# A gated sum of chunked attention and a long convolution on one core: another written order of the same steps

## The chip, the core and the metric

The kernel runs on one core of a Trainium2 chip. The core has TensorE (matmuls, "PE" in the profile; "PEld" is its weight load), Vector ("DVE"), Scalar ("ACT"), GpSimd ("POOL") and SyncE ("SP", which issues all DMAs here). The metric is device time in microseconds of one execution. Three runs of the kernel before gave 381.07, 383.3 and 385.4 us; the median is 383.3.

## What is computed

The reference takes x (2048 tokens, 512 columns, bf16) and mixes two results by a gate per token:

```python
g = sigmoid((x * gate_w).sum(-1, keepdims=True))
return g * A(x) + (1 - g) * B(x)
```

A is attention over four segments of 512 tokens with 32 heads of 16 columns. Within a segment it is causal softmax attention; what earlier segments left is read from a running state M (16x16 per head, from phi(k) and v, phi(t) = t+1 for t > 0, else exp(t)) and mixed in per head by sigmoid(beta). Then `@ wo`.

B is a state-space convolution: per column d a kernel K[d, l] = Re sum_n C P^l dB with 128 complex states n, and y = causal convolution of x with K over 2048 tokens (an FFT of length 4096 in the reference), plus x * Dskip.

## The kernel before

**Attention.** Each segment s and group hg of 8 heads has the steps: projections `pk`, `pq` (four 128x512 matmuls each), five score blocks `sc` that fill PSUM banks 0 to 3 together, one Scalar exponential of 128x2048 per block (L1021), products with v (`pv`, 17 columns per head so that the sum of weights falls out), `nrm` on Vector (L993 to L996: reciprocal, product, product), the state step `st`/`sm`, the state's read `mem` (L1071 to L1075) and a transpose `oT`. Per segment there are also `xT` (transposes of x), `tok` (v) and `gate`.

**The convolution's kernel.** `prep` computes exp(dt*A) by exponential and sine; `pow0`, `pow1` square it again and again for the two halves of the columns (L751 to L753), `pwc` converts each power (L759 to L763). For each quarter c of the columns, `tab`c builds two tables F and G of powers, by 13 complex products, each of three Vector instructions:

- L1118: table = table entries x one part of the power
- L1121: t2 = the same entries x the other part
- L1125: table = table + t2

The third reads both earlier ones; the second doesn't read the first. `lag`c then multiplies F and G by 256 small matmuls of 128x20 and evicts the result. F and G exist once, so `tab`(c+1) may begin to overwrite them only when `lag`c's matmuls are done.

**The convolution.** `xl1` makes the first level of a transform of x and stores it in a scratch tensor scr_Z in DRAM. The tail reads it back in 16 steps t: `Zx` loads 256 KB, `X` are two matmuls, their result is copied with its two 64-partition halves swapped by two DMAs (sb<-sb), `CT` loads 448 KB of constants (c_DN), `K` transforms the convolution's kernel, `Y` (L1220) is the product, `V` transforms back and is stored in V2 by a DMA. Zx and CT have three buffers each. `fin` adds attention's result `@ wo` and the skip term into a PSUM bank, `fir` adds the last level over all of V2, an eviction multiplies by the gate, and the result is stored. The tail's buffers M2 and V2 lie over F and G, those of CT and Zx over the powers, so the `X` steps follow `lag3`.

**What sets the order.** `build_graph` records 1679 steps, each with its dependencies and the tiles it touches. The string ORDER lists them by number; a letter behind the number (a or v) puts a free eviction on Scalar (L240) or Vector (L241). `Sched.replay` walks the string: each engine's program is the listed order of its own steps, and SP's queue the listed order of the DMAs. A tile takes a slot of its pool when its first step is walked and gives it back after its last. `Pool.take` chooses the slot that became free longest ago, `Psum.take` the bank (or pair) free longest ago out of 4 to 7, and banks 0 to 3 only before the first score block and after the last. `Sched.emit` then puts a semaphore wait before a step for each producer that isn't known to be done, also for a producer on the same engine, other than TensorE.

```python
o.alld = list(o.deps)
for T in o.wt:
    o.alld += list(T.prev)
...
if d.eng == o.eng and o.eng == "PE":
    continue
if know.get(d.sem, 0) >= d.val:
    continue
o.waits.append(d)
```

Of the kernel before, what the change touches and what calls it, by code (L numbers as in the profile page):

```python
# [24 lines left out]
class Pool:  # L25


    def __init__(self, name, addr, size, n=1, phase=1):
        self.name, self.addr, self.size, self.n, self.phase = name, addr, size, n, phase
        self.free = [(0, i, ()) for i in range(n)]  # L30
        self.left = 0
        self.last = {}
        self.blockers = ()
        self.idx = -1

    def take(self, tile, now):
# [10 lines left out]
    def give(self, tile, now):  # L47
        self.free.append((now, tile.slot, tuple(tile.users)))
        self.last[tile.slot] = tile.users
        self.left -= 1  # L50


class Psum:


    def __init__(self):
        self.free = {b: (0, ()) for b in range(8)}
        self.wide = self.begun = self.ended = 0

    def take(self, tile, now):  # L60
        best = None
        low = self.begun == 0 or self.ended == self.wide or len(tile.banks) == 1
        for cand in tile.banks:
            if all(b in self.free and (low or b > 3) for b in cand):
                t = max(self.free[b][0] for b in cand)
                if best is None or t < best[0]:
                    best = (t, cand)
        cand = best[1]
        tile.prev = [o for b in cand for o in self.free[b][1]]
        for b in cand:  # L70
            del self.free[b]
        tile.slot, tile.cand = cand[0], cand
        self.begun += len(tile.banks) == 1

    def give(self, tile, now):
        self.ended += len(tile.banks) == 1
        for b in tile.cand:
            self.free[b] = (now, tuple(tile.users))
# [34 lines left out]
class Sched:  # L113
# [37 lines left out]
    def ps(self, width=1, dt=F32, banks=None):  # L151
# [5 lines left out]
        self.psum.wide += len(banks) == 1  # L157
# [91 lines left out]
    def replay(self, order):  # L249
# [4 lines left out]
        for now, (i, e) in enumerate(order):  # L254
            o = self.ops[i]
            if o.alts:
# [12 lines left out]
            for T in o.tiles:  # L269
                T.nuse -= 1  # L270
                if T.nuse == 0:
                    T.pool.give(T, now + 1)
# [100 lines left out]
192 53 0 204 8 394 9 14 12 13 54 10 56 11 55a 15 22 28 57v 16 3 26 23a 1 24 17 27v 25a 1234 29 30 202 376 32 31 33 4  # L373
34 252 203a 18 35 36 44 2 199 253a 37 39 20 38 40 249 19 41 200a 42 21 43 201 211 172 5 173 7 218 219 45 6 47 207 48
46 49 52 58 209 174 50 175 61a 51 220 67v 68 69 66 176 59 60 72 212v 70 239 62 64 63 240 71 188 82 84 65 205 85a 83 78
241 86 87 189 190 191 193 76 227 194 97a 228 77 210a 98 99 94 208v 195 229 73v 213 74 75 95 96 106 108 235 90 206a 236
107 109v 118 221 120 237 119 133v 134 135 110 111 121a 196 79v 222 130 80 122 223 123 88 131 132 91a 234 144 224 238
89 102 242 177 243 178 142 225 100 179 226 230 143 145a 157v 154 156 103a 158 155 159 197 101 250a 114 112 1240 146
115a 147 113 124 126 104 127a 105 125 136 138 116 214 117 137 139a 150 180 148 166a 149 160 162 181 163a 161 92 169a
93 198 128 1002a 170 1003a 171 1008 1004a 129 251 1005a 215 261 1006a 1007 1241a 1010 262 1011 151a 1012 182 1009 1242  # L380
263 1016 183 184 1235 185 186 187 1017 1018 1236a 1022 265 1243a 1023 266 1244 1024 1237 267 1013 295 1014 1015 216
164 165 1238a 81 140 270 141 296a 271 231 1239 232 233 217 272 1025 292 377 1026 293a 278 378a 279 1027 379 280 1255
264 268 1038 269 273 274 380a 282 275 276 283 294 244 245 254 246 284 1245 152 153 1019 247 1020 1021 1028 248a 306
1029 255 307 1246a 1030 256 1247 257 308 277 1034 281 258 1037 1248a 311 1249 259 312 260 1039 1250 313 1252 1035 336
1276 1036 1251a 302 1253a 303 333 337a 167 1254 168 304 1031 1266 1268 1032 285 286 287 288 334a 289 319 1033 1267a
320 290 321 305 1040 309 291v 310 314 1256 1041 1258 1042 1269a 323 1043 1257a 324 1044 1270 1259a 1045 297 318 335
325 322 315 1260 316 1046 317 1047 1048 1049 298 345 1050v 346 299 1051 347 300 1052 1053 1054 301 1060v 1061v 1062v
1063a 1064v 349 1055a 1068 350 1069 1056 1070 1261 1074 351 1263 1057 326 1075 327 1058 1076 1078 1059 328 329 330
1262a 354 1080 1264a 355 1081 331 1265 356 386 1082 348 1083 352 353 332a 362 1084 387a 363 389 364 1271 1085 357 390a
358 366 359 1272a 367 360 393 391 1273 388 1092 338 591 368 1277 392 1093 1274a 408 339 1094 1275 409 1278a 1279 410  # L390
397 340 341 1280v 1065 1281 1066 1067 412 398a 1071 413 1072 342 1073 414 399 1077 343 344 443 1079 1086 400a 361 1087
425 444a 426 365 1088 427 401 1089 395 1090 402a 1091 429 396a 430 445 1098 411 431 1099 446 1100 1101 1282 1102 369
370 1103 447a 415 609 371 417 1283a 372 450 418 373 448 1095 374 419 1284 381 416 449 382 375v 493 1096 1285a 462 383
384 1286 463 494a 385 424 495 420 464 1097 403 1292 428 432 421 433 422 434 404 435 458 436 1293a 459 423 1104 405 460
1105 406 1106 1107 1109 1108v 1110 475 476 1111 477 1112 461 1113v 407 1118v 1114 1124 1294 1119v 1120v 1121a 1287
1115 1122v 479 1295a 1126 480 1127 1116 1288a 1128 1289 1117 1132 481 465 1133 496 1296 1134 1297 1138 466 1139 1290a
467 497a 468 1291 1140 592 498 500 1141 594 469 806 499 1142 593a 523 524 1143 470 525 1298 1123 1125 1129 1299a 1130
515 1131 595a 516 471 472 473 1300 1135 517 1136 541 1137 1144 1145 1301a 451 1146 542a 1302 1303 452 1147 1305 1304a
1148 1306a 474 506 1149 1307 507 543 1308 453 508 478 454 1310 1156 455 1157 482 1158 483 456 1309a 527 484 1311a 485
528 486 457 1312 437 529 1150 544 1313 438 439 545a 440 510 1314a 511 548 1151 546 441 512 487 1315 547 442v 488 509  # L400
489 1316a 490 565 566 1317 1152 513 567 514 491 522 1153 526 501 530 492a 531 1154 556 502 557 601 558 532 533 534 518
1155 549 602a 560 1159 550 561 1160 604 1161 562 503 504 1162 603 551 1163 552 1164 519 520 605a 1165 521 573 1166a
# [944 lines left out]
```

## Time and profile before

| | before |
|---|---|
| runs | 381.07, 383.3, 385.4 us |
| profiled execution: time, span | 381.07 us, 381.1 us |
| granted TensorE clock, mean | 0.870 |
| Vector instructions, Scalar instructions | 627, 322 (3 of them table loads) |
| matmuls | 4268 |
| DMA: bytes, mean rate | 36.07 MB, 95 GB/s |
| longest releaser of Scalar's evictions (L240) | TensorE, 42.7 us in 47 waits |
| longest releaser of Scalar's exponentials (L1021) | TensorE, 26.4 us in 33 waits |
| median from issue to landing: c_DN, scr_Z read, sb<-sb | 5.5, 5.1, 5.1 us |

"Busy" is time in which an engine executes an instruction; the remainder is idle time, which the profile puts down to whatever semaphore came last. The profile's evictions and matmuls go through helpers, so one line (L646, L240, L241) stands for many steps; steps are told apart by shape and time.

### The profile page before, as it was taken

The page shows a single profiled execution, that of the slowest core. Times are in us where ns is not written, and L with a number is a line of the kernel's source. Part 1 is how long each engine was busy: PE and PEld are TensorE (multiplying, and loading weights), DVE is VectorE, ACT ScalarE, POOL GpSimd, SP SyncE. Part 2 cuts the span into 40 slices and gives each one's busy share as a digit, 9 for nine tenths or more (in the row PEclk, how much of TensorE's full clock was granted, in tenths as well). Part 3 has the DMA queues.
Part 4 walks back from the last instruction along what each step waited for, and adds up shares of the span by engine and source line. Part 5 has one row for each costly group of instructions (what it writes and reads, how often), then busy time and mean ns, then how long its engine had stood idle before and what let it go on. Part 6 is the DMA issues. An engine that isn't in the chain of part 4 may idle for free.

```text
span 381.1 us, 9878 instructions
## 1 busy us (share of the span) xinstructions
PE 298.8 (78%) x4268; PEld 170.4 (45%) x4268; DVE 275.0 (72%) x627; ACT 275.1 (72%) x322; POOL 3.2 (1%) x9
## 2 busy tenths in 40 slices
PE   3856167877696768879955899999969888788994
PEld 3314024455353534556532657655323433334551
DVE  0699999996998499978996352989768687644011
ACT  4599999788995589797965485789947786544242
POOL 1000000000000000000000000000000000000000
PEclk9965559689997586999968696999989999999998
DMA  7900002121200061101005500002797587663113
GB/s 180 321 15 1 3 28 84 64 104 49 84 29 29 3 184 58 57 3 21 2 2 156 204 3 2 2 2 56 233 248 210 172 245 210 187 174 110 34 75 146
DMA packets 25755, 36.07 MB, mean 95 GB/s; under 512 B 9200, under 2 KB 13808, under 8 KB 25584
## 3 DMA queue, kind: packets, MB, share of 16 engines
q1 hardware_dynamic: 25712, 35.45, 31.0%
q8 instruction: 33, 0.54, 0.6%
q14 instruction: 10, 0.08, 0.1%
HBM read 20.10 MB, written 6.29 MB: 69 GB/s over the span
## 4 chain that ended last, share of the span: by engine, by line
DVE 40%; PE 34%; DMA 14%; ACT 5%; issue 5%; SPq 2%; ACTq 0%
PE psum L646 33%; DVE sb L1118 8%; DVE sb L1125 8%; DVE sb L1121 7%; DMA sb<-c_DN 5%; DMA sb<-sb 5%; DMA sb<-scr_Z 3%; DVE sb L241 3%; ACT sb L1021 2%; DVE sb L996 2%; SPq L236 2%; DVE sb L753 1%; DMA sb<-in_B_C_im_dram 1%; DVE sb L752 1%; DVE sb L763 1%
## 5 line engine op out<-in xcount | busy, mean ns | idle before, releaser
L646 PE MATMUL psum<-sb 128*128 128x17 bf16 (+12 forms) x4132 | 287.2, 239 | 68.9 <-ACT sb L1021 21.6
L646 PEld LDWEIGHTS psum<-sb 128*128 128x128 bf16 (+3 forms) x4132 | 159.9, 100 | 193.9 <-issue 46.8
L1021 ACT ACTIVATE sb<-psum 128x2048 bf16<-128x2048 f32 x80 | 150.3, 1879 | 26.9 <-PE psum L646 26.4
L240 ACT ACTIVATE sb<-psum 128x512 bf16<-128x512 f32 (+2 forms) x143 | 85.0, 623 | 49.5 <-PE psum L646 41.4
L241 DVE CAST sb<-psum 128x512 bf16<-128x512 f32 (+1 forms) x66 | 43.7, 675 | 34.1 <-PE psum L646 29.4
L1118 DVE TENSOR_TENSOR sb<-sb 128x512 bf16<-128x512 bf16 (+3 forms) x52 | 35.8, 690 | 0.8
L1125 DVE TENSOR_TENSOR sb<-sb 128x512 bf16<-128x512 bf16 (+3 forms) x52 | 34.7, 669 | 1.5
L1121 DVE TENSOR_TENSOR sb<-sb 128x512 bf16<-128x512 bf16 (+3 forms) x52 | 35.5, 685 | 0.1
L1220 DVE TENSOR_TENSOR sb<-sb 128x1024 bf16<-128x1024 bf16 x32 | 21.7, 687 | 7.7 <-ACT sb L240 4.7
L244 DVE TENSOR_SCALAR sb<-psum,sb 128x512 bf16<-128x512 f32 x5 | 3.8, 751 | 21.4 <-PE psum L646 21.4
L243 ACT ACTIVATE sb<-psum,sb 128x512 bf16<-128x512 f32 x11 | 7.6, 687 | 14.8 <-PE psum L646 14.8
L996 DVE TENSOR_TENSOR sb<-psum,sb 128x256 bf16<-128x256 f32 x32 | 13.4, 423 | 0.9
L1033 DVE TENSOR_TENSOR sb<-sb 128x1024 bf16<-128x1024 bf16 (+1 forms) x20 | 11.5, 573 | 0.0
L751 ACT ACTIVATE sb<-sb 128x512 f32<-128x512 f32 x18 | 11.0, 626 | 0.1
L684 PE MATMUL psum<-sb 128*128 128x128 bf16 x64 | 5.8, 254 | 6.1 <-DMA sb<-c_ident 4.7
L993 DVE RECIPROCAL sb<-psum 128x16 f32<-128x16 f32 x32 | 8.0, 250 | 1.2 <-PE psum L646 1.1
L943 DVE TENSOR_SCALAR sb<-sb 128x512 bf16<-128x512 bf16 x16 | 5.6, 349 | 4.4 <-ACT sb L240 4.4
L759 ACT ACTIVATE sb<-sb 128x512 bf16<-128x512 f32 x14 | 8.7, 620 | 0.0
L952 ACT ACTIVATE sb<-sb 128x512 bf16<-128x512 bf16 x12 | 7.6, 634 | 1.3 <-PE psum L646 1.0
L1075 DVE TENSOR_TENSOR sb<-psum,sb 128x512 bf16<-128x512 f32 x12 | 8.3, 689 | 0.3
L1071 DVE SCALAR_TENSOR_TENSOR sb<-psum,sb 128x32 f32<-128x32 f32 x12 | 2.2, 184 | 8.3 <-PE psum L646 8.3
L684 PEld LDWEIGHTS psum<-sb 128*128 128x128 bf16 x64 | 4.8, 115 | 7.1 <-DMA sb<-c_ident 4.7
(65 smaller groups left out, 116.3 us busy)
## 6 DMA issues: line engine op xcount, KB each, us to landing
sb<-c_DN SPq DMA_DIRECT2D x16, 448.0 KB, 5.5
sb<-in_A_x_dram SPq DMA_DIRECT2D x8, 512.0 KB, 3.7
scr_Z<-sb SPq DMA_DIRECT2D x16, 256.0 KB, 2.0
sb<-scr_Z SPq DMA_DIRECT2D x16, 256.0 KB, 5.1
sb<-sb SPq DMA_DIRECT2D x32, 128.0 KB, 5.1
sb<-sb SPq DMA_DIRECT2D x16, 256.0 KB
out_dram<-sb SPq DMA_DIRECT2D x8, 256.0 KB, 2.1
sb<-c_M SPq DMA_DIRECT2D x1, 1024.0 KB, 6.4
```

The source lines that it names most:

```text
L240: fa = lambda e: e.activation(dst(), src(), ACT.Copy)
L241: fd = lambda e: e.tensor_copy(dst(), src())
L646: mm = lambda e, o_, l, r_, st, sp, **kw: e.matmul(o_, lhsT=l, rhs=r_, start=st, stop=sp, skip_group_check=True, **kw)
L684: i = e.transpose(ap(P, t2 * 512 + k * 128, n=128), ap(xks, (2 * hb + t2) * 512 + k * 128, n=128), ap(ident, n=128))
L751: op("ACT", ("As", 512), lambda e, sq=sq, Z=Z: e.activation(ap(sq, n=512), ap(Z, n=512), ACT.Square), r=[Z], w=[sq], key=PW[h] + PWS * k)
L996: op("DVE", ("V1", 256), lambda e: e.tensor_tensor(ap(o1, gi * 16, [[128, 4], [32, 4], [1, 16]]), ap(T, dims=[[68, 4], [17, 4], [1, 16]]), ...
L1021: o = op("ACT", ("Ax", 2048), lambda e, P=P, pT=pT: e.activation(ap(pT, n=2048), ap(P, n=2048), ACT.Exp, scale=0.25), r=[P], w=[pT])
L1033: op("DVE", ("V2", 128 * nb), lambda e, pT=pT, dims=dims: e.tensor_tensor(ap(pT, dims=dims + [[1, 128]]), ap(pT, dims=dims + [[1, 128]]), ...
L1118: op("DVE", ("V2", 256 * n), lambda e: e.tensor_tensor(run(tile, ne, dst, 1), run(tile, ne, src, sstep), ap(pw, cl * 512, [[2, 128], [0, n ...
L1121: op("DVE", ("V2", 256 * n), lambda e: e.tensor_tensor(run(t2, n, 0, 1), run(tile, ne, src, sstep), ap(pw, cl * 512 + 256, [[2, 128], [0, ...
L1125: op("DVE", ("V2", 256 * n), lambda e: e.tensor_tensor(D_(), D_(), ap(t2, n * 128, [[-n * 128, 2], [2 * n, 64], [1, 2 * n]]), ALU.add), r= ...
L1220: op("DVE", ("V2", 1024), lambda e, Y=Y, XAB=XAB, K3=K3, pi=pi: e.tensor_tensor(ap(Y, dims=[[512, 2], [1, 512]]), ap(XAB, pi * 512, [[1024 ...
```

## The change

The graph of steps, the pools and their addresses stay. The string ORDER is replaced by another one in which all 1679 steps stand in another order, some free evictions stand on the other engine, and every tile's slot or bank is written out behind the number of the step that first touches it. `take` no longer chooses; it uses the written slot.

```diff
-        self.free = [(0, i, ()) for i in range(n)]
+        self.free = {i: () for i in range(n)}
...
-    def take(self, tile, now):
+    def take(self, tile, k):
...
-        best = min(self.free, key=lambda f: (f[0], f[1]))
-        self.free.remove(best)
-        tile.slot = best[1]
-        tile.prev = list(best[2]) + prev
+        tile.slot = k
+        tile.prev = list(self.free.pop(k)) + prev
...
 class Psum:
-    def take(self, tile, now):
-        best = None
-        low = self.begun == 0 or self.ended == self.wide or len(tile.banks) == 1
-        for cand in tile.banks:
-            if all(b in self.free and (low or b > 3) for b in cand):
-                t = max(self.free[b][0] for b in cand)
-                if best is None or t < best[0]:
-                    best = (t, cand)
-        cand = best[1]
-        tile.prev = [o for b in cand for o in self.free[b][1]]
+    def take(self, tile, k):
+        cand = tile.banks[k]
+        tile.prev = [o for b in cand for o in self.free.pop(b)]
...
-        for now, (i, e) in enumerate(order):
+        for now, (i, e, slots) in enumerate(order):
...
-                    T.pool.take(T, now + 1)
+                    T.pool.take(T, next(slots))
...
-ORDER: 192 53 0 204 8 394 9 14 12 13 54 10 56 11 55a 15 22 28 57v 16 3 26 23a 1 24 17 27v 25a 1234 ...
+ORDER: 14/0 28/0 9/4 204/1 8/3 0/0 22/5/0 10/0 53/0 56/3 11/5 24/0/1 23v 29/10 1/0 3/0 54/4 16/0 ...
```

What the strings come to shows on each engine's own list. Vector, around the second quarter's tables (name of the step, xN for N instructions of it in a row):

```
before: tabc1x4 tab1.1x3 tab1.3x3 tab1.4 nrm0.2.1x3 tab1.5x3 tab1.6x3 nrm0.3.0x3 ...
after:  tabc1x2 tab1.1x2 tabc1 tab1.0x2 pwc1.6 tab1.0 tab1.1 tab1.3 tab1.2 tab1.3 tab1.2 tab1.3 ...
```

SP's queue begins before with x, the identity, A_re, A_im, log_dt, C_re, C_im, B_re, B_im, wq; after with log_dt, A_im, A_re, the identity, B_re, x, B_im, two small masks, wk, C_im. Free evictions up to the last `lag3` matmul: of 512 columns, 66 on Scalar and 7 on Vector before, 69 and 4 after; of 1024 columns 9 and 2 before, 6 and 5 after; converted powers (L759, L760) 14 and 6 before, 11 and 9 after.

More of the change, by code (lines that the diff above doesn't have):

```diff
@@ L41, in take, with give @@
                 prev += v
-        best = min(self.free, key=lambda f: (f[0], f[1]))
-        self.free.remove(best)
-        tile.slot = best[1]
-        tile.prev = list(best[2]) + prev
-    def give(self, tile, now):
-        self.free.append((now, tile.slot, tuple(tile.users)))
+        tile.slot = k
+        tile.prev = list(self.free.pop(k)) + prev
+    def give(self, tile):
+        self.free[tile.slot] = tuple(tile.users)
         self.last[tile.slot] = tile.users
@@ L56, in __init__, with give @@
     def __init__(self):
[L57 to L71 removed]
+        self.free = {b: () for b in range(8)}
+    def take(self, tile, k):
+        cand = tile.banks[k]
+        tile.prev = [o for b in cand for o in self.free.pop(b)]
         tile.slot, tile.cand = cand[0], cand
[L73 to L76 removed]
+    def give(self, tile):
         for b in tile.cand:
[L78 removed]
+            self.free[b] = tuple(tile.users)
 class Part:
@@ L271, in replay @@
                 if T.nuse == 0:
-                    T.pool.give(T, now + 1)
+                    T.pool.give(T)
             done.append(o)
@@ L1305, in build_kernel @@
         for w in ORDER.split():
-            order.append((int(w.rstrip("av")), "ACT" if w[-1] == "a" else "DVE"))
+            w = w.split("/")
+            order.append((int(w[0].rstrip("av")), "ACT" if w[0][-1] == "a" else "DVE", [int(v) for v in w[1:]]))
         S.replay(order)
```

150 lines of the change are left out of this document (84 added, 66 removed).

## The prediction

> **What bounds the kernel now.** I read the profile in four steps: the page's first part and its chain, then busy time by stage, then the Vector engine's timeline inside one stage, then the list of waits for the last stage.
>
> ```profile
> PE 298.8 (78%) x4268; PEld 170.4 (45%) x4268; DVE 275.0 (72%) x627; ACT 275.1 (72%) x322; POOL 3.2 (1%) x9
> ...
> DVE 40%; PE 34%; DMA 14%; ACT 5%; issue 5%; SPq 2%; ACTq 0%
> ```
>
> No engine is full, and the chain that ended last changes hands: Vector, then TensorE, then DMA. So I cut the span where the work changes. The only matmuls of shape 128x20 are those of the four table steps ("lag0" to "lag3"); in the timeline they end near 89, 131, 171 and 211 us. The first matmul of step X0 stands near 263, the last V matmul near 353.
>
> ```profile
> core 0: us, PE busy (x) PEld busy (x) DVE busy (x) ACT busy (x) POOL busy (x), PEclk, DMA share, GB/s
> 10.00:89.00 79.00, 51.69 (x762) 27.26 (x761) 70.72 (x191) 69.54 (x94) 0.00 (x0) 0.72 0.22 73
> 89.00:131.00 42.00, 32.14 (x639) 19.08 (x632) 34.80 (x76) 32.33 (x38) 0.66 (x1) 0.85 0.13 44
> 131.00:171.00 40.00, 31.66 (x638) 19.69 (x634) 36.16 (x79) 35.82 (x39) 0.00 (x0) 0.86 0.22 72
> 171.00:211.00 40.00, 30.19 (x720) 19.07 (x704) 33.40 (x69) 28.49 (x32) 0.66 (x1) 0.87 0.18 57
> 211.00:263.00 52.00, 50.53 (x725) 34.05 (x721) 32.60 (x88) 37.55 (x34) 0.00 (x0) 0.87 0.09 29
> 263.00:353.00 90.00, 75.95 (x675) 34.97 (x675) 62.49 (x119) 59.54 (x75) 0.00 (x0) 0.98 0.70 196
> 353.00:381.00 28.00, 22.43 (x143) 12.45 (x141) 3.75 (x5) 7.97 (x12) 0.00 (x0) 0.94 0.24 85
> ```
>
> To 211 us Vector is fullest (33 to 71 us busy per row), Scalar close behind, TensorE loose: call it stage 1. From 211 to 263 TensorE is full. From 263 to 353 TensorE works 76 of 90 us while the DMA engines are 70% busy, and after 353 it is TensorE alone. The tail's buffers lie over the tables' buffers, so it can't begin before lag3: a microsecond saved in stage 1 is a microsecond off the end.
>
> Inside stage 1 the spacing of Vector's instructions matters:
>
> ```profile
> 105.36 0.41 DVE L1118 TENSOR_TENSOR sb<-sb 128x256 bf16<-128x256 bf16 x1
> 105.69 0.40 DVE L1121 TENSOR_TENSOR sb<-sb 128x256 bf16<-128x256 bf16 x1
> 106.12 0.42 DVE L1125 TENSOR_TENSOR sb<-sb 128x256 bf16<-128x256 bf16 x1
> ...
> 131.65 0.49 DVE L241 CAST sb<-psum 128x320 bf16<-128x320 f32 x1 [4.20 <-PE psum L646]
> ```
>
> Columns are start, duration, instruction, and in brackets idle time and its releaser. L1121 doesn't need L1118's result and starts 0.33 us after it, 0.08 before its end. L1125 adds both products and starts 0.03 us after L1121's end. Over all neighbouring Vector pairs whose other inputs were ready, the medians are +0.034 us where the second reads the first's result (204 pairs) and -0.084 us where it doesn't (267 pairs). A dependent neighbour costs 0.118 us. The last row is another loss: Vector has run out of work and waits 4.2 us for lag1's matmuls.
>
> **The change, part by part.** Both written orders, engine by engine, hold 4268 matmuls, 151 DMAs and the same steps; Vector goes from 627 to 626 and Scalar from 319 to 320 instructions (the page's 322 include 3 table loads). So the work stays and I price places.
>
> *Vector's neighbours.* Up to the last lag3 matmul, 162 of Vector's 416 instructions before directly follow the one they read; after, 23 of 423. That is 139 x 0.118 = 16.4 us. In place of runs of three (product, product, sum) two or three tables' steps, powers and normalisations alternate. Moved evictions and the seven more instructions ahead of lag3 add 2.2 us by the mean durations (512 columns: Vector 0.686, Scalar 0.601; 1024: 0.692 against 1.024). By duration plus spacing, Vector needs 73.9, 35.6, 37.1, 34.1 us between the lag marks, 180.7 in all; after 65.1, 33.6, 33.0, 34.3, 166.0. Scalar, with its own median of -0.104 us between independent neighbours, needs 161.7 before and 60.0, 34.6, 32.5, 32.5 = 159.6 after. The larger of the two per stage sums to 180.7 and 167.0: 13.7 us less.
>
> The Trainium skill, "VectorE: DVE Perf Modes", section "The DRAIN you can't avoid", speaks against this: it says every Vector instruction is followed by a drain which leaving out semaphores doesn't avoid ("the semaphore costs nothing extra here", measured on a row of copies). By that rule spacing would gain nothing and the sum would end near 376. The rows above differ from it by the 0.118 us.
>
> *Stalls in stage 1.* It lasts 200.6 us from 10, against 180.7 of Vector work: 19.9 of stalls, most where a table is done and the next must wait for its matmuls (4.20 above, 2.15 before 89.4). Between the last step of one table and the first of the next, before has 2.4, 3.4 and 3.7 us of other Vector work, after 6.0, 6.1 and 6.0. That is 8.6 us more cover. Against it, Vector and Scalar are now within 4% of each other; Scalar had 39 us free in this stage and each can now hold the other. I take 3 us of new stalls net: **-11 us**. From below: Scalar keeps most of its free time, -4; from above: cover works fully, -18.
>
> *The head.* SP issues the tables' parameters (A_im, A_re) ahead of x, so Vector's first useful eviction is no longer behind x's transposes (6.60 us) and the third parameter's load (9.56). Their transposes need the identity, now fourth in the queue where it was second: two issues of 0.5 us later. Parameters ready near 7.5 instead of 10.2; the exponent and sine steps behind them are a chain with little beside it. I take **-1.5**, between 0 and -3.
>
> *211 to 263.* TensorE's issue time (fastest tenth of each kind of step) from lag3 to X0 is 44.6 us before and 42.6 after, as 2 us more stands ahead of lag3: **-2**, between 0 and -4.
>
> *263 to 353.* Here loads end late:
>
> ```profile
> PE psum L646 <- DMA sb<-c_DN: 8.4, 4, 3.1
> PEld psum L646 <- DMA sb<-c_DN: 4.5, 2, 2.5
> PE psum L646 <- DMA sb<-scr_Z: 3.0, 3, 1.3
> ```
>
> Each line gives total us, times, longest. A CT tile (c_DN) can load only when the last V matmul on its slot is done and lands 5.5 us after issue (median of the DMA list); Zx (scr_Z) takes 5.1; the half-swap of X and its two neighbours some 7.5 from X's matmul to V's. I measured how much TensorE work each order puts between release and use. Shortfalls below 5.5, 6 and 7.5 us add up to 15.0 + 10.6 + 9.2 = 34.8 us before and 12.0 + 8.5 + 4.4 = 24.9 after. Before, the stage took 89.4 us for 69.3 of issue time: 20.1 of stalls for 34.8 of shortfall. The same ratio gives 14.4 for 24.9: 5.7 less; issue time falls 1.2. Since 70% DMA share leaves little room for loads to land faster, I take **-5** of these 6.9; between +4 and -9.
>
> *After 353.* TensorE has 24.1 us of issue time behind the last V instead of 22.6, as fewer output steps are opened ahead: **+1.5**, between 0 and +3.
>
> **Sum**: -11 - 1.5 - 2 - 5 + 1.5 = -18 us on the profiled execution's 381.1 us (its time and its span agree; nothing lies around it): 363. That execution is the quickest of three with median 383.3, so the same step on the median gives 365. Ends of the terms added: -34 and +3, unlikely together.
>
> **Rivals.**
> *Scalar takes over stage 1.* For it: Scalar needs 159.6 us in order and waits for TensorE before its evictions (42.7 us over the span). Against it: 39 us of slack existed. Stage 1 then gives 4 instead of 11: 372.
> *Spacing is worth nothing.* If a start held back by 0.118 us is made up within the next instructions, Vector's 16.4 us aren't there to win and the 11 us of stage 1 go: 376. Against it are the 204 pairs, each a later start that nothing after it takes back. (The section named above states this outcome.)
> *The swaps come late* (the slower side). In the new order the SP queue's swaps of X stand nearer their use: measured in TensorE work between the written place of the issue and the product that reads it, tiles fall short of 5 us by 28 us in all, against 12.4 before. X7, X15 and X0 have 0 to 1 us. If the written place is when SP really gets to them, held by loads ahead that wait for TensorE, stage 263 to 353 grows by up to 15.6 where I have it shrink by 5, and 365 becomes 386. It decides once more than about 18 us of the shortfall shows, as Vector stands in front of Y while the other evictions queue behind it. Against it: from X's matmul to V's the new order has more distance, and no long wait stands ahead of X7 on SP. Ten one-bank tiles now also sit in banks 0 to 3, which the scores need whole (none did in the tail before); at one 0.69 us eviction each that pushes the same way.
> *More than forecast.* Stage 1 loses nothing to new stalls and the tail gains its 9: 352 to 357.
> *Nothing moves within 1%*: gains and late loads cancel.
>
> **Numbers.** Forecast (358 to 369) 0.47; Scalar 0.18; spacing nothing 0.06; more 0.09; within 1% 0.08; slower 0.12 by late swaps. Rounded: faster by over 1% 0.80, within 1% (about what three runs between 381.1 and 385.4 can tell) 0.08, slower 0.12. The range leaves out the slower case and a little at the low end: 351 to 381.
>
> **What would show it.** Right: the last 128x20 matmul ends at 195 to 203; before 211, neighbouring Vector rows show starts before the previous end almost everywhere and no wait of 4 us at a table's end; Scalar's busy share in stage 1 rises to match Vector's; waits on c_DN and scr_Z fall from 15.9 to 10 to 12 us; the last V stands 6 to 8 us nearer to X0. Wrong: lag3 still near 210 with Vector idle (stage 1 bound by the table, matmul, table loop or by Scalar), or DVE L1220 waiting long on sb<-sb in the tail.

## The result, and the profile after

The changed kernel takes 348.86 us (median; 347.06 to 350.03), against 384.09 us for the kernel before (four runs, 381.07 to 385.4). The ratio is 0.909 with a 95% interval of 0.904 to 0.914: about 35 us faster, where 18 were forecast, and outside the range of 351 to 381. The sign was right and the size half. Ratios here and below leave out executions in which the chip ran slower as a whole, so they can differ a little from the ratios of the medians.

The page of the kernel after, busy time and the chain that ended last:

```profile
PE 280.7 (81%) x4225; PEld 165.3 (48%) x4268; DVE 256.3 (74%) x626; ACT 269.1 (78%) x323; POOL 3.2 (1%) x9
...
PE 31%; DVE 30%; ACT 22%; DMA 10%; issue 5%; SPq 1%; DVEq 0%
```

The trace lacks 43 of the 4268 matmuls. Scalar's share of the chain has gone from 5% to 22% and Vector's from 40% to 30%: the chain now passes among three engines. The busy time by stage, with the columns of the table shown of before (stretch and length in us, busy us of TensorE, its weight load, Vector, Scalar and GpSimd, granted clock, DMA share, GB/s), cut at Vector's first `prep` instruction, at the last matmul of each lag step (to within 0.3 us), at the first X and at the last V:

```profile
7.00:74.50 67.50, 48.06 (x781) 27.92 (x793) 65.84 (x190) 64.75 (x87) 0.00 (x0) 0.90 0.32 96
74.50:107.40 32.90, 28.47 (x629) 17.31 (x636) 32.07 (x80) 32.58 (x39) 0.67 (x1) 1.00 0.16 54
107.40:142.50 35.10, 28.72 (x686) 19.65 (x689) 34.21 (x83) 34.69 (x40) 0.00 (x0) 1.00 0.20 67
142.50:179.50 37.00, 28.84 (x657) 19.16 (x660) 31.14 (x72) 30.79 (x33) 0.66 (x1) 0.93 0.22 64
179.50:227.50 48.00, 46.60 (x627) 31.10 (x633) 25.20 (x72) 37.89 (x37) 0.00 (x0) 0.88 0.12 41
227.50:317.00 89.50, 76.50 (x713) 36.90 (x723) 60.52 (x122) 61.18 (x80) 0.00 (x0) 0.98 0.68 194
317.00:345.30 28.30, 22.51 (x142) 12.51 (x142) 6.66 (x9) 5.30 (x8) 0.00 (x0) 0.99 0.26 94
```

In the second and third rows Vector and Scalar are busy for 97 to 99% of the time. With the same cuts in the trace of before (10.2, 89.3, 131.6, 171.7, 210.6, 262.8, 352.8 and 381.1 us) the stretches compare so:

| stretch, us | before | after | difference | forecast |
|---|---|---|---|---|
| start to Vector's first `prep` (head) | 10.2 | 7.0 | -3.2 | -1.5 |
| to the last lag3 matmul (stage 1) | 200.4 | 172.5 | -27.9 | -11 |
| to the first X | 52.2 | 48.0 | -4.2 | -2 |
| to the last V (tail) | 90.0 | 89.5 | -0.5 | -5 |
| to the end | 28.3 | 28.3 | 0 | +1.5 |
| span | 381.1 | 345.3 | -35.8 | -18 |

(The profiled run's time is 347.06 us, 1.8 above its span; all later runs lie 1.7 to 1.9 above theirs.)

Vector's timeline inside the second quarter's tables, after (start, duration, instruction, idle time and releaser in brackets):

```profile
88.86 0.68 DVE L1129 TENSOR_TENSOR sb<-sb 128x1024 bf16<-128x1024 bf16 x1
89.46 0.25 DVE L997 RECIPROCAL sb<-psum 128x16 f32<-128x16 f32 x1
89.63 1.16 DVE L1122 TENSOR_TENSOR sb<-sb 128x2048 bf16<-128x2048 bf16 x1
90.70 0.16 DVE L998 TENSOR_TENSOR sb<-sb 128x16 f32<-128x16 f32 x1
90.82 1.23 DVE L1129 TENSOR_TENSOR sb<-sb 128x2048 bf16<-128x2048 bf16 x1
...
107.20 0.30 DVE L226 COPY sb<-sb 128x256 bf16<-128x256 bf16 x1 [0.63 <-PE psum L650]
```

(L1122, L1129, L997, L998 and L226 are L1118, L1125, L993, L994 and L241 of before.) Steps of a table and of a normalisation alternate, and each row starts 0.04 to 0.09 us before the end of the one above it. The last row is the wait at the end of this table (the first copy into the next one, behind the last lag1 matmul): 0.63 us, where the eviction shown of before waited 4.20.

The list of waits in stage 1, Vector's own, first of before and then of after (total us, times, longest):

```profile
DVE sb L241 <- PE psum L646: 9.8, 5, 4.2
DVE sb L943 <- ACT sb L240: 3.6, 2, 2.9
```

```profile
DVE sb L226 <- PE psum L650: 1.6, 3, 0.6
DVE sb L929 <- PE psum L650: 1.1, 1, 1.1
```

To split stage 1, I summed what each of an engine's gaps exceeds 0.06 us by, called that its idle time, and called all else its **need** (work and spacing). Scalar's two table loads count as idle, TensorE's gaps that end in no wait that the profile shows ("issue") don't. The last few us of the stage, in which Vector waits for lag3's matmuls (3.8 before, 4.4 after), fall into the need. For Vector, 200.4 us were 185.0 of need and 15.4 of idle time; 172.5 are 169.1 and 3.4. So 15.9 us came out of the need and 12.0 out of the stalls. Scalar's idle time fell from 31.9 to 12.5 us, TensorE's from 43.0 to 27.2.

### The profile page after: what moved, and what is told of

Its sections match the earlier page's. It is cut to its first block, busy times and chain, and to the rows that moved or that the text cites. A ratio compares the mean times of both kernels' runs of the same rounds, so it can differ in the third digit from the quotient of the medians.

```text
span 345.3 us, 9849 instructions
## 1 busy us (share of the span) xinstructions
PE 280.7 (81%) x4225; PEld 165.3 (48%) x4268; DVE 256.3 (74%) x626; ACT 269.1 (78%) x323; POOL 3.2 (1%) x9
## 4 chain that ended last, share of the span: by engine, by line
PE 31%; DVE 30%; ACT 22%; DMA 10%; issue 5%; SPq 1%; DVEq 0%
PE psum L650 30%; ACT sb L1025 11%; DVE sb L1125 7%; DVE sb L1122 7%; DVE sb L1129 6%; DMA sb<-c_DN 6%; ACT sb L225 6%; ACT sb L755 3%; DVE sb L226 2%; ACT sb L763 2%; DVE sb L1224 2%; DMA sb<-in_A_x_dram 1%; SPq L221 1%; DMA sb<-sb 1%; DVE sb L1000 1%
## 5 line engine op out<-in xcount | busy, mean ns | idle before, releaser
L650 PE MATMUL psum<-sb 128*128 128x17 bf16 (+11 forms) x4089 | 270.8, 231 | 50.7 <-ACT sb L1025 23.2
L650 PEld LDWEIGHTS psum<-sb 128*128 128x128 bf16 (+3 forms) x4132 | 155.9, 98 | 163.1 <-issue 37.1
L1025 ACT ACTIVATE sb<-psum 128x2048 bf16<-128x2048 f32 x80 | 151.4, 1892 | 18.8 <-PE psum L650 18.0
L225 ACT ACTIVATE sb<-psum 128x512 bf16<-128x512 f32 (+2 forms) x155 | 89.4, 628 | 26.1 <-PE psum L650 22.7
L226 DVE CAST sb<-psum 128x512 bf16<-128x512 f32 (+1 forms) x51 | 33.5, 673 | 28.0 <-PE psum L650 23.3
L1122 DVE TENSOR_TENSOR sb<-sb 128x512 bf16<-128x512 bf16 (+3 forms) x52 | 35.2, 683 | 0.1
L1125 DVE TENSOR_TENSOR sb<-sb 128x512 bf16<-128x512 bf16 (+3 forms) x52 | 35.1, 684 | 0.1
L1129 DVE TENSOR_TENSOR sb<-sb 128x512 bf16<-128x512 bf16 (+3 forms) x52 | 33.5, 660 | 0.0
L228 ACT ACTIVATE sb<-psum,sb 128x512 bf16<-128x512 f32 x7 | 4.7, 686 | 18.0 <-PE psum L650 18.0
L229 DVE TENSOR_SCALAR sb<-psum,sb 128x512 bf16<-128x512 f32 x9 | 6.7, 750 | 14.0 <-PE psum L650 13.8
L1000 DVE TENSOR_TENSOR sb<-psum,sb 128x256 bf16<-128x256 f32 x32 | 13.2, 414 | 0.6 <-PE psum L650 0.2
L997 DVE RECIPROCAL sb<-psum 128x16 f32<-128x16 f32 x32 | 7.9, 249 | 5.6 <-PE psum L650 5.5
L1037 DVE TENSOR_TENSOR sb<-sb 128x1024 bf16<-128x1024 bf16 (+1 forms) x20 | 11.1, 572 | 1.1 <-ACT sb L1025 0.9
L226 DVE COPY sb<-psum 128x1024 bf16<-128x1024 bf16 x5 | 3.4, 687 | 6.3 <-PE psum L703 6.3
L756 DVE TENSOR_TENSOR sb<-sb 128x256 f32<-128x256 f32 x18 | 7.6, 420 | 0.1
L905 ACT ACTIVATE sb<-psum 128x512 bf16<-128x512 bf16 x12 | 7.4, 615 | 0.3 <-PE psum L902 0.3
L757 DVE SCALAR_TENSOR_TENSOR sb<-sb 128x256 f32<-128x256 f32 x18 | 7.5, 421 | 0.0
```

What stands on the lines that cost most here:

```text
L225: fa = lambda e: e.activation(dst(), src(), ACT.Copy)
L226: fd = lambda e: e.tensor_copy(dst(), src())
L650: mm = lambda e, o_, l, r_, st, sp, **kw: e.matmul(o_, lhsT=l, rhs=r_, start=st, stop=sp, skip_group_check=True, **kw)
L1000: op("DVE", ("V1", 256), lambda e: e.tensor_tensor(ap(o1, gi * 16, [[128, 4], [32, 4], [1, 16]]), ap(T, dims=[[68, 4], [17, 4], [1, 16]]), ...
L1025: o = op("ACT", ("Ax", 2048), lambda e, P=P, pT=pT: e.activation(ap(pT, n=2048), ap(P, n=2048), ACT.Exp, scale=0.25), r=[P], w=[pT])
L1037: op("DVE", ("V2", 128 * nb), lambda e, pT=pT, dims=dims: e.tensor_tensor(ap(pT, dims=dims + [[1, 128]]), ap(pT, dims=dims + [[1, 128]]), ...
```

## The experiments

My theory after the result: stage 1 is paced by Vector in the new order; it became shorter by spacing (some 13 to 16 us), by other work between two tables, and by parameters that arrive earlier; the tail hardly matters. The rivals: the granted clock (0.80 in stage 1 before, 0.94 after), the engines of the evictions, the slots, the tail's order. In the diffs below a list is Vector's or SP's own order, by the names of the steps, xN for N instructions in a row. "Stage 1" is always cut as above, and idle times are the sums of gaps. "Over the changed kernel" is against its 348.86 us; the kernel before, run beside each group, had medians of 383.6 to 386.1 us, so a difference of 2 us between groups means little.

### Spacing undone in the new order

82 of Vector's chains are put back into runs, each at the place of its last instruction; 99 instead of 23 instructions ahead of lag3 follow the one they read.

```diff
-tab1.0 tab1.0 pwc1.6 tab1.0 tab1.1 tab1.3 tab1.2 tab1.3 tab1.2 tab1.3 st0.3 nrm0.2.1 tab1.4 tab1.4 ...
+pwc1.6 tab1.0x3 tab1.1x3 tab1.2x3 tab1.3x3 st0.3 tab1.4x3 nrm0.2.1x3 ...
```

> The new order with one thing undone: 82 of Vector's chains (a table step's product, product, sum; a normalisation's three instructions) are put back into runs, each at the place of its last instruction. Up to lag3, dependent neighbours on Vector go from 23 to 99 (before: 162). Everything else keeps its order and engine. Theory (spacing is worth 0.118 us each, Vector sets stage 1): 76 x 0.118 = +9 us, so about 358 us (355 to 361). Rival (spacing is worth nothing, the gain is in the stalls and the head): 347 to 351.

Measured: 361.29 us (358.3 to 363.74), ratio 0.943 [0.933, 0.952]; 12.4 us over the changed kernel. Stage 1 takes 185.7 us, 13.2 more. Its row:

```profile
7.00:192.70 185.70, 134.78 (x2740) 85.58 (x2766) 171.11 (x422) 164.35 (x198) 1.33 (x2) 0.91 0.23 71
```

Vector's busy time rises from 163.25 to 171.11 us for the same 422 instructions, its need by 10.1 and its idle time from 3.4 to 6.5. 76 more dependent neighbours at 0.118 us are 9.0 us; most of the rest is the idle time, 3.1 us more. So in the new order spacing is worth its full price and a little more.

### Spacing added to the old order

105 of Vector's instructions move forward by up to 8 places in the order of before, so that 39 dependent neighbours are left of 162.

```diff
-nrm0.2.1x3 tab1.5x3 tab1.6x3 nrm0.3.0x3
+nrm0.2.1 tab1.5 nrm0.2.1 tab1.5 nrm0.2.1 tab1.5 tab1.6x2 tab1.9 tab1.6 nrm0.3.0 pk1.0 nrm0.3.0 tab1.9 nrm0.3.0
```

> The kernel before with one thing done: 105 Vector instructions are moved forward by up to eight places to stand between two dependent neighbours. Dependent neighbours up to lag3 fall from 162 to 39; all other engines keep their order, slots are chosen as before. Theory: 123 x 0.118 = -14.5 us in Vector's need; with the stalls of before unchanged about 370 us (366 to 374). Rival (Vector only waits longer for Scalar and for the table matmuls): above 379.

Measured: 390.59 us (388.66 to 393.9), ratio 1.025 [1.014, 1.036]: slower than before. Stage 1:

```profile
10.00:214.50 204.50, 143.11 (x2675) 85.84 (x2692) 165.38 (x415) 166.03 (x200) 1.31 (x2) 0.81 0.19 62
```

Vector is busy for 165.4 us in place of 175.1 and its need is 8.4 us less (14.5 by the law), so the spacing worked on Vector itself, and yet the stage is 4.2 us longer. Vector's idle time went from 15.4 to 28.0 us: 17.4 behind TensorE (15 waits) and 10.6 behind Scalar (20 waits), nearly all at instructions that I hadn't moved (normalisations, state steps, lag evictions). Two readings were left: either Vector's saving turns into waits for the others whatever I do, or my moves had delayed what the others wait for.

The moves also had a side effect: the rule of before chooses slots by the written order, and so it gave 211 PSUM tiles another bank and 73 SBUF tiles another slot, which can bring waits of its own.

A gentler version tells the two readings apart: 47 instructions, the second of a dependent pair in the tables, powers and parameters only, put 1 to 3 places later; 96 dependent neighbours left. Here every PSUM bank stays and 18 SBUF tiles change their slot.

```diff
-tab1.6x3 nrm0.3.0x3
+tab1.6x2 nrm0.3.0 tab1.6 nrm0.3.0x2
```

> The kernel before with a gentler spacing: 47 times the second of two dependent neighbours (of the tables, powers and parameters only) is put one to three Vector instructions later, so that what TensorE and Scalar wait for comes earlier, never later. Dependent neighbours before lag3 fall from 162 to 96: 66 x 0.118 = 7.8 us less of Vector's need. If e2 gained nothing only because its moves delayed what the other engines wait for: -5 to -8 us, 376 to 380. If the order of TensorE and Scalar holds stage 1 of before whatever Vector does: 382 to 388.

Measured: 380.78 us (377.01 to 383.23), ratio 0.998 [0.993, 1.003], no difference.

```profile
10.00:206.50 196.50, 139.21 (x2675) 84.31 (x2692) 170.06 (x414) 165.62 (x200) 1.33 (x2) 0.81 0.20 64
```

In the profiled execution stage 1 is 3.8 us shorter: Vector's need is 5.6 us less (66 places at 0.118 us would be 7.8) and its idle time 1.8 more. Over ten runs the interval leaves at most 2.6 us of that, and none is as likely. So the first reading holds in part, as half or more of the saving doesn't arrive; the first version did harm besides, by its harsher moves or by the other banks, which isn't separated further.

### Vector loaded, in both orders

The second product of 40 table steps is computed twice, first into an unread half of t2. That is 16.4 us more work on Vector and nothing else.

```diff
-            op("DVE", ("V2", 256 * n), lambda e: e.tensor_tensor(run(t2, n, 0, 1), ...
+            def twice(e):
+                for off in ([1024, 0] if n <= 4 else [0]):
+                    i = e.tensor_tensor(ap(t2, off, ...
```

In the order of before:

> The kernel before with a load on Vector: in the 40 table steps that take at most 4 entries, the second product is computed twice, the first time into a free half of its tile (12 x 0.32 + 16 x 0.34 + 12 x 0.60 = 16.4 us more of Vector's time, all before lag3; nothing else moves). Theory (stage 1 before is paced by TensorE and Scalar, Vector has 15 us of idle time in it): the load hides in part, +4 to +10 us. Rival (Vector paces stage 1 before, as the prediction had it): +16 us, about 401.

Measured: 401.46 us (400.45 to 404.96), ratio 1.044 [1.035, 1.053], 15.3 us more than before beside it.

```profile
10.00:227.10 217.10, 146.46 (x2699) 86.73 (x2696) 192.54 (x455) 166.50 (x200) 1.32 (x2) 0.77 0.19 60
```

In the new order:

> The new kernel with the same load on Vector, 16.4 us. Theory (Vector paces stage 1 in the new order, 3.4 us of idle time in it): +14 to +18 us over the new kernel, 363 to 367. Rival (Scalar paces it): +5 to +10, 354 to 359.

Measured: 365.93 us (363.7 to 368.44), ratio 0.950 [0.941, 0.959], 17.1 us over the changed kernel.

```profile
7.00:197.80 190.80, 143.15 (x2765) 86.68 (x2766) 180.63 (x462) 164.67 (x198) 1.31 (x2) 0.89 0.23 69
```

Stage 1 grows by 16.7 and by 18.3 us. Vector's work is on the path in both orders, one for one. Whether added work on Scalar would lengthen the new order as well wasn't tried. With the section above this gives an asymmetry: in the old order more work on Vector costs its full price, and less returns under half of its own.

### The cover between tables undone

In the new order, 19 Vector instructions that stand between two tables move behind 8 instructions of the next table.

```diff
-pwc1.6 pwc1.2 pk0.3 nrm0.2.0 lag0 nrm0.2.0 pwc1.4 gate nrm0.2.0 pwc1.9 st0.2 xl1.7 gate pwc1.2 st0.2 tabc1x2 ...
+pwc1.6 pk0.3 nrm0.2.0 lag0 nrm0.2.0x2 tabc1x2 tab1.1x2 tabc1 tab1.0x2 pwc1.6 pwc1.2 pwc1.4 gate pwc1.9 st0.2 ...
```

> The new order, but 19 of Vector's instructions that stand between the end of one table and the begin of the next are moved behind eight Vector instructions of the next table: 2.6, 3.6 and 5.3 us of other work are left there (6.0, 6.1, 6.0 in the new order; 2.4, 3.4, 3.7 before). Theory (this work covers the wait for the table matmuls): Vector waits again there, +4 to +7 us: 352 to 356. Rival (the table matmuls are done in time anyway): 347 to 351.

Measured: 354.45 us (351.79 to 359.05), ratio 0.918 [0.910, 0.926]; 5.0 us more than the kernel with other slots below, which ran beside it. Stage 1 grows by 7.9 us to 180.4, mostly at the first two borders (36.2 for 32.6 us and 38.5 for 35.2 between the lag marks). Vector's waits there:

```profile
DVE sb L226 <- PE psum L650: 6.4, 7, 3.2
DVE sb L927 <- PE psum L650: 2.3, 2, 1.9
```

The wait for the table's matmuls is back (3.2 us at the longest, where the changed kernel has 0.6), and Vector's idle time goes from 3.4 to 11.1 us. The edit takes away 6.6 of the 18.1 us of cover (2.6, 3.6 and 5.3 us are left), and 7.7 us of idle time come back.

### SP's first loads in the old order

```diff
-log_dt A_im A_re identity B_re x B_im mask mask wk ...
+x identity A_re A_im log_dt C_re C_im B_re B_im wq wk ...
```

> The new order with SP's first 23 loads in the order of before (x, identity, A, log_dt, C, B, then weights), all else as new. Theory: Vector's work starts 3 us later and is full from there to lag3, so +3 us: about 352 (350.5 to 354). Rival (the head is hidden behind the parameter chain): 347 to 350.

Measured: 352.46 us (350.57 to 353.6), ratio 0.922 [0.914, 0.929], 3.6 us more. The head is only 0.4 us longer, but the stretch to lag0 takes 73.4 us for 67.5. Scalar's waits in it, of this kernel:

```profile
ACT sb L824 <- DMA sb<-in_A_beta_dram: 3.0, 1, 3.0
ACT sb L723 <- DVE sb L722: 2.0, 1, 2.0
ACT sb L1025 <- PE psum L650: 1.5, 2, 1.2
```

The first line isn't in the changed kernel: the exponential of beta stands in Scalar's written order before beta has arrived, and everything behind it waits. Vector's idle time in stage 1 is 9.1 us for 3.4. The order of the loads is worth its few microseconds in stage 1's stalls, not at the start where I had looked.

### Engines of the evictions

The new order, with 109 of the 267 free evictions (40 of them ahead of lag3) on the engine that before gives them. Letters a and v name the engine:

```diff
-14/0 28/0 9/4 204/1 8/3 0/0 22/5/0 10/0 53/0 56/3 11/5 24/0/1 23v ...
+14/0 28/0 9/4 204/1 8/3 0/0 22/5/0 10/0 53/0 56/3 11/5 24/0/1 23a ...
```

> The new order with every free eviction on the engine it had before (109 of the free evictions change engine; their places in the order stay). Theory now (run e2 gave no gain though Vector's need fell, so stage 1 before was paced by TensorE and Scalar waiting for each other, and the new order fills Scalar's gaps): evictions that were placed into Scalar's gaps now stand elsewhere, Scalar's and Vector's idle time in stage 1 grow by 8 to 20 us together: 355 to 365. Rival (an eviction costs 0.60 to 0.69 us on either engine and only the sum counts): 347 to 351.

Measured: 390.03 us (386.23 to 391.61), ratio 1.011 [1.002, 1.019]: the whole gain is gone. Waits in stage 1, and the row of its tail:

```profile
ACT sb L1025 <- PE psum L650: 10.2, 15, 1.9
...
DVE sb L226 <- PE psum L650: 5.9, 6, 2.0
...
DVE sb L756 <- ACT sb L763: 2.9, 1, 2.9
```

```profile
248.80:356.20 107.40, 82.95 (x713) 37.97 (x722) 63.19 (x126) 58.64 (x73) 0.00 (x0) 0.90 0.58 162
```

The head hardly changes (Vector's first `prep` product stands at 7.4 us for 7.0). In stage 1 Scalar's exponentials (L1025) wait 10.2 us for TensorE, where the changed kernel's wait 4.7, Vector's evictions and copies (L226) 5.9 for 1.6, and one squaring step of the powers (L756) 2.9 us for a conversion on Scalar. Vector idles 21.6 us in this stage, which takes 189.2. The tail takes 107.4 us. Neither engine has much more work (Vector's and Scalar's tail rows differ by under 3 us from the changed kernel's), so it is the time at which the evictions come; which of the 109 do the harm wasn't taken apart.

The other way round, the order of before with the new kernel's engines:

```diff
-192 53 0 204 8 394 9 14 12 13 54 10 56 11 55a 15 22 28 57v 16 3 26 23a ...
+192 53 0 204 8 394 9 14 12 13 54 10 56 11 55v 15 22 28 57v 16 3 26 23v ...
```

> The mirror of e5: the order of before, with every free eviction on the engine it has in the new kernel (109 change). If the new choice of engines is worth something by itself: faster than before, 365 to 380. If engine and place only work together, as e5 suggests: slower by 5 to 40 us, 389 to 425.

Measured: 395.89 us (395.58 to 398.77), ratio 1.043 [1.033, 1.054]. Stage 1 takes 206.1 us, the tail 95.0; idle times in stage 1 are 23.0 (Vector), 40.5 (Scalar) and 50.0 us (TensorE), all above before. So the choice has no worth of its own. Order and engines fit each other, and either one with the other's partner is slower than before.

### Slots

341 SBUF tiles of the new order (at 331 steps) take the slot that became free longest ago, as before's rule does. The PSUM banks stay as written.

```diff
-14/0 28/0 9/4 204/1 8/3 0/0 22/5/0 10/0 53/0 56/3 11/5 ...
+14/0 28/0 9/0 204/0 8/1 0/0 22/5/0 10/2 53/0 56/3 11/3 ...
```

> The new order and engines; every SBUF slot is the one that became free longest ago, as before chose it, in place of the written one (331 steps get another slot; PSUM banks as written). All theories that put the gain into the order: 347 to 351. Rival (the written slots take waits away): 353 or more.

Measured: 349.42 us (347.14 to 352.35), ratio 0.909 [0.901, 0.917], a span of 345.4. The written SBUF slots are worth nothing that can be measured.

### The tail

The new order up to lag3, the order of before for all that follows (with before's engines: 69 evictions change theirs); Vector's list right behind lag3:

```diff
-pk2.3x2 sm2.0 nrm2.1.0 fq2.0 nrm2.1.0x2 mem2.0x3 fq2.1 nrm2.1.1x3 diag gate3 ...
+diag fq2.0 fq2.2 sm2.0x2 oT1.3 fq2.1 pq2.3 pk2.3 fq2.3 mem2.0x3 nrm2.1.0x3 ...
```

> The new order up to the last lag3 matmul, and everything left after it in the order of before. Theory (31 of the 35 us are won before lag3; the stretch after it gives 4 and the tail nothing): about 352 to 353 us. Rival (the new tail order also gives, as forecast 5 to 7 us, and the old one loses it): 356 to 361.

Measured: 350.36 us (350.12 to 351.56), ratio 0.917 [0.911, 0.924]; 1.5 us over the changed kernel. The tail takes 89.2 us with the old order and 89.5 with the new one. All but a microsecond or two of the gain was made ahead of the tail.

What holds the tail, then? Its loads of constants are cut: for 13 of the 16 tiles only 8 of 1792 columns are brought (the result is another one).

```diff
+            nct = 1792 if t < 3 else 8
-            S.dma(lambda CT=CT: ap(CT, n=1792), lambda t=t: hC[t], ...
+            S.dma(lambda CT=CT, nct=nct: ap(CT, n=nct), lambda t=t, nct=nct: hC[t][:, 0:nct], ...
```

> The new kernel, but 13 of the 16 loads of c_DN bring 8 of 1792 columns; their steps compute with what the slot still holds, so the result is another one. 5.9 MB of 20 MB of the tail's transfers are gone and the load always lands early. Theory of the prediction (the tail waits for its loads): the 10.4 us of waits on c_DN go and the other loads land sooner, tail 89.5 to about 78, so 337 to 340. Rival (the tail is a chain through TensorE, evictions and the swaps, and a wait on c_DN only stands in for the next one): 344 to 349.

Measured: 343.05 us (two runs, 339.7 and 346.39); the profiled span is 337.9 us.

```profile
226.00:309.70 83.70, 75.29 (x713) 36.20 (x723) 60.40 (x122) 61.06 (x80) 0.00 (x0) 1.00 0.53 137
```

In this execution, the quicker of the two, the tail is 5.8 us shorter. The loads cost it that, by their bytes or by when they are issued. The next kernel keeps all the bytes, and gives the loads a fourth buffer in place of three; each load from the fourth on is issued at the place where the one before it stood.

```diff
-    CTP = mkpool("CT", 3584, 3, 2)
+    CTP = mkpool("CT", 3584, 4, 2)
...
-CT0 CT2 xl1.15 Zx1 lag3x4 ld_M2 Zx4 Zx0 ... X2 CT3 V0.1 X3x2 Zx6 V1.1 CT7 CT4 ...
+CT0 CT2 CT3 xl1.15 Zx1 lag3x4 ld_M2 Zx4 Zx0 ... X2 CT7 V0.1 X3x2 Zx6 V1.1 CT4 CT5 ...
```

> The new kernel with four buffers for c_DN in place of three, and each load from the fourth on issued where the one before it stood (one V step earlier). If the tail waits for loads because they are issued late (e8 took 7 us off by leaving most of them out): -3 to -6 us, 343 to 346. If they are late because the DMA engines are 68% busy in the tail and only the bytes count: 347 to 350.

Measured: 344.8 us (339.21 to 346.38), ratio 0.899 [0.888, 0.911]; span 337.4.

```profile
225.00:309.20 84.20, 75.18 (x713) 36.16 (x723) 60.34 (x122) 61.10 (x80) 0.00 (x0) 1.00 0.72 201
```

In this execution the tail is 5.3 us shorter with the same bytes, and no wait on c_DN is left in the list; the DMA share rises from 0.68 to 0.72. So the loads were late because they were issued late. What it is worth in the kernel's time is less clear. The execution is the quickest of six, 5.6 us under their median, and 2.5 us of its lead lie ahead of the tail, where the granted clock was higher (shown below). The medians differ by 4.1 us, about 1%, and the two intervals overlap. It is the fastest version here with the same result.

### The clock

Six more matmuls of 128 columns after each `pv` of segments 0 to 2, into columns that nothing reads, raise TensorE's activity and with it the granted clock.

```diff
+                if s < 3:
+                    for _ in range(6):
+                        i = mm(e, ap(T, 384, n=128), ap(ident, n=128), ap(ident, n=128), False, last)
```

In the order of before:

> The kernel before with six more matmuls of 128 columns at the end of each product with v of segments 0 to 2, into columns of its bank that nobody reads (60 calls' worth per segment; 0.06 us each at full clock). It raises TensorE's work in stage 1 so that its granted clock (0.70, 0.84, 0.87, 0.87 between the lag marks; 0.88 to 1.00 in the new kernel) should rise. If the low clock is what stretches stage 1 before: faster by 5 us or more in spite of the added work. If the clock is only a mark of the waiting: slower by 2 to 15 us.

Measured: 397.99 us (394.52 to 403.48), ratio 1.033 [1.022, 1.044].

```profile
10.00:216.70 206.70, 162.50 (x3123) 107.33 (x3123) 175.95 (x415) 166.16 (x200) 1.32 (x2) 0.90 0.20 62
```

In the new order:

> The same six matmuls per product in the new kernel, where the granted clock is already 0.88 to 1.00: it shows what they cost by themselves. Both theories: +2 to +12 us, 351 to 361.

Measured: 368.02 us (366.37 to 368.87), ratio 0.955 [0.948, 0.962], 19.2 us over the changed kernel.

```profile
7.00:196.40 189.40, 156.56 (x3209) 108.63 (x3210) 164.81 (x422) 163.61 (x197) 1.32 (x2) 0.95 0.23 70
```

In the old order the clock in stage 1 rises from 0.80 to 0.90, most of the way to the changed kernel's 0.94, and the stage becomes 6.3 us longer. In the new order the clock can't rise (0.94 to 0.95), and the same matmuls cost 16.9 us there. The 10.6 us between the two could be what the better clock gave back in the old order, or the room that TensorE had there (its idle time fell by 10.3 us in the old order, by 2.8 in the new one). The runs don't separate these. What they show is that a higher clock got in this way is no net gain; by this comparison its share in the 35 us is at most about 10 and may be nothing.

Kernels whose compute lists are the same, but which were granted different clocks, narrow this. Up to lag3 four others (other slots, the tail of before, short loads, four buffers) have the changed kernel's lists. At 0.97, 0.91, 0.95 and 0.93 their stage 1 took 172.7, 173.9, 171.3 and 173.1 us, for 172.5 at 0.94. In this range the clock goes with 1 to 3 us of stage 1; before's 0.80 lies outside it. The kernel with the chains put back, at 0.91 as well, took 185.7 us, so its loss isn't the clock's. From lag3 to the first X, where TensorE is full, it counts. The kernel with four buffers has the same lists there too:

```profile
180.00:225.00 45.00, 43.74 (x625) 29.76 (x631) 25.22 (x72) 37.87 (x37) 0.00 (x0) 0.96 0.13 46
```

It took 45.0 us at 0.96 where the changed kernel took 48.0 at 0.88.

### What wasn't tried

Taking one engine's list from the new order and another's from the old would have split the stalls among the engines' orders. Every such mix of TensorE's, Scalar's, Vector's and SP's lists holds a cycle of waits, so none was run. The written PSUM banks weren't undone either; what they are worth in the 35 us is open.

## Why the prediction was right in sign and short by half

**Vector's need in stage 1 was right.** Forecast -14.7 us (180.7 to 166.0), measured -15.9. The law behind it holds in the trace of after: dependent neighbours start 0.034 us after the end of the one before (54 pairs), others 0.083 us before it (421 pairs). Undoing 76 of the places cost 12.4 us, for 9.0 by the law.

**The stalls were the step that failed**: "I take 3 us of new stalls net". Measured is a loss of 12.0 us of stalls. I had counted 8.6 us of cover and let a fuller Scalar eat more than all of it. The cover is there (7.7 us of Vector's idle time come back when 6.6 us of it are taken away), the order of the first loads takes another 5.7 us of idle time out of the same stage, and the new stalls didn't come: Scalar's idle time fell as well, from 31.9 to 12.5 us. So stage 1 gave -27.9 where I wrote -11, beyond even my "-18" for cover that works fully, because that bound took less than all of the cover (13.7 of need and 8.6 of cover would have made 22) and none of the loads. I had reasoned that two engines within 4% of each other must hold each other up. With an order written so that each result is ready when its reader's turn comes they don't. That this fit is fragile is shown by the evictions on other engines (+41 us). The parts undone one by one (spacing 13.2, cover 7.9, loads 6.4 us, of stage 1 and the head together) come to 27.5 of their 31.1 us, if they add. That wasn't tried, and the engines of the evictions, which undone alone cost more than the whole gain, show that parts of this order need not add.

**The head** was mis-sized, -3.2 for -1.5, a little past my end of -3. Vector's first `prep` at 7.0 is what I had written ("near 7.5 instead of 10.2"), but I discounted it for a chain with little beside it. That discount was wrong: the first `pow` step stands 6.8 us earlier (at 12.8 us for 19.6).

**211 to 263** was mis-sized: -4.2 for -2. TensorE's busy time there fell by 3.9 us (50.53 to 46.60). I had counted the work that now stands ahead of lag3 (44 matmuls) at the fastest tenth of each step, while the granted clock was 0.88. And I had overlooked 48 matmuls of 17 columns (`pv` of segment 3) that leave the stretch the other way, to behind X0: in the tail, where the weight loads go from 675 to 723 and the busy time of such matmuls from 9.5 to 10.9 us. So some 1.4 of the 4.2 us were handed to the tail and not saved.

**The tail failed too**: "The same ratio gives 14.4 for 24.9: 5.7 less". It stayed: 89.5 us. The waits on c_DN and scr_Z did fall, from 15.9 to 13.0 us, a little less than I wrote (10 to 12). The list of waits in the tail of after:

```profile
PE psum L650 <- DMA sb<-c_DN: 5.5, 4, 2.9
...
PEld psum L650 <- DMA sb<-c_DN: 4.9, 2, 3.4
...
DVE sb L226 <- DMA sb<-sb: 4.0, 1, 4.0
```

But those on the swaps grew from 9.1 to 10.2 us, 4.0 in a single one, so that all DMA waits fell by 1.8 us while the 48 matmuls above came in; the tail became 0.5 us shorter. Counting shortfalls at the written places didn't tell what they cost. My remark that a DMA share of 70% leaves little room was wrong as well: with a fourth buffer the share is 72%, no load of c_DN is waited for, and the tail of that execution is 5.3 us shorter.

**The end** was 28.3 us in both, for +1.5. Behind the last V stand 144 matmuls in both orders. The +1.5, and the "issue time falls 1.2" of the tail, fit a last V taken to be V15.1; in the new order eight matmuls of `fin` and V15.0 follow it, some 1.5 us that still belong to the tail.

**The rivals.** *Scalar takes over* did not happen: stage 1 gave 27.9 us and not 4, and work added to Vector alone lengthens it one for one. *Spacing is worth nothing* is refuted in the new order by the run with the chains put back. So the rule of the Trainium skill ("VectorE: DVE Perf Modes", "The DRAIN you can't avoid") that synchronisation between neighbours "costs nothing extra here" doesn't cover this kernel: a neighbour that reads the result costs 0.118 us. In the old order spacing brought nothing that could be told from none, yet for another reason: Vector was less busy, and the saved time became waits. I had not asked whether the term depends on the rest of the order. *The swaps come late* shows as 10.2 us of waits for 9.1, far from the 18 us from which it would decide. *More than forecast* named the cause of stage 1 ("loses nothing to new stalls") but joined it to a gain in the tail that didn't come.

Of what I wrote would show it: no wait of 4 us at a table's end (0.63) and Scalar's busy share matching Vector's (94% and 95%) came true; lag3 at 195 to 203 us didn't (179.5), nor did the last V come nearer to X0.

## What to carry to other kernels

When in-order engines (here Vector and Scalar) are each 80 to 90% busy and wait for one another, price a new order in two separate terms, the fullest engine's need and the idle time that is left. The second can go almost to nothing; bound it by all the idle time there is, not by the one cover that was counted. Relieving one engine's list alone may give next to nothing (Vector's in the old order: ratio 0.998), and half of a new order (its places without its engines, or the reverse) can be worse than none. When a stage waits for loads at a DMA share of 0.7, try an earlier issue or one more buffer before concluding that the DMA engines are full.

## What the runs showed of the hardware that I had not expected

- An engine can be on the path for added work and not for removed work: 16.4 us more on Vector made stage 1 of the old order 16.7 us longer, while 5.6 us less need left the kernel at a ratio of 0.998 [0.993, 1.003].
- A clock raised from 0.80 to 0.90 by filler matmuls didn't pay for them: the kernel became 12 us slower, and 19 us in the denser order.
- In the stretch where TensorE is full, the same lists took 48.0 us at a granted clock of 0.88 and 45.0 at 0.96. In stage 1, the changed kernel's lists took 173.9 us at 0.91 and 171.3 to 172.7 at 0.94 to 0.97.
- The DMA engines at a share of 0.68 were not the limit of the tail; in the profiled executions the same bytes issued earlier ran at 0.72, 201 GB/s in place of 194, and the tail took 84.2 us for 89.5.
